# Batch 0's attention weights as zero-padded bands: 8 products over 128 keys for a unit instead of 24, and a new order

## The chip, the cores and the metric

The kernel runs on one core of one Trainium2 chip. The metric is the device time of one execution in microseconds (us). Three runs of the kernel before took 899.35, 900.56 and 900.95 us; the median is 900.56 us.

## The reference, cut to what matters

Attention over 8 batches, 8 heads, 576 positions, head size 64, with a causal window of 32 keys (heads 0 to 3) or 32 keys at a stride of 4 (heads 4 to 7), and then one expert of a mixture layer on the 4608 tokens: two fp32 products with a rational function between them.

```python
scores = scale * np.matmul(q, k.transpose(0, 1, 3, 2))
mask_plain = (rel >= 0) & (rel < window)                                # window = 32
mask_dil = (rel >= 0) & (rel < window * dilation) & (rel % dilation == 0)  # dilation = 4
attn = np.exp(scores - np.max(scores, axis=-1, keepdims=True))
attn = attn / (np.sum(attn, axis=-1, keepdims=True) + 1e-09)
attn_out = np.matmul(attn, v)
# x: (4608, 512), w_in: (512, 2048), w_out: (2048, 512)
h = x @ w_in
g = (a[0] + a[1] * h + a[2] * h * h + a[3] * h * h * h) / (1 + |b[0]| * |h| + |b[1]| * h * h + 1e-6)
out = g @ w_out
```

## The kernel before

**Attention.** The host reorders the positions of heads 4 to 7, so that both kinds of window become 32 neighbouring keys. A batch is 6 units; a unit is 4 heads (two pairs, named h and e below) by 192 queries. Its 192 queries are six blocks of 32, (r, i) with r in 0..1 and i in 0..2, and each block sees 64 keys, its own 32 and the 32 before. So all weights of a unit are 128 rows (4 heads by 32 queries) by 6 blocks of 64 keys, 384 columns. For a unit, `scores` makes 24 products of 64 by 32 by 64; `max`, `sub`, `exp`, `sum`, `recip` and `norm` are the softmax on DVE, ACT and POOL; `transposes` turns the 384 columns in three transposes on TensorE into one PSUM tile, `place` copies it to SBUF, and `av` multiplies with the values. In batch 0 `av` writes the result with the head's dimensions on the partitions, ready for the expert: one product of 64 keys, 64 dimensions and 32 queries for each block and head, 24 for a unit. The two r lie on the two halves of the partitions, so the values are stored for every block with its 64 keys, twice in all (`NV` = 768 columns).

**The expert.** Tokens are taken 512 at a time (9 groups, c = 0 to 8; the last is the 64 last positions of all batches), hidden features 128 at a time (16 slices), which makes 144 tiles. fp32 is split into a high and a low part, and each product is three (`mm` calls on xh, xl, wi; gh, gl, wo): `h` is 12 matmuls of 128x512, then a chain of some 12 operations on ACT, DVE and POOL gives g, and 4 `out` groups of 3 matmuls add to the results. The order of the runs is batch 0 with slices 0 to 7, batch 1 with all, batch 0 with 8 to 15, then batches 2 to 7 and the rest. Batch 0's six units must be done before the first tile; their q, k and values lie in the buffers of late weights (wi10 to wi15, wo10 to wo15). The weights come from HBM as 64-bit numbers and take five steps each on ACT, DVE and POOL.

**The order.** A planner (`Plan`) records every operation with the engines it may run on, and `ORDER`, a list of operation numbers, says in which order the first 1,700 or so are issued; behind the list a greedy rule with the ranks `LATE`, `DUE` and `SLACK` goes on. Each engine works its queue in that order. SP issues every DMA, in one queue. Where the planner thinks TensorE idle early on, `keep_busy` puts in matmuls that add nothing; `BUSY_FIRST` of them stand before the first scores.

**The last tiles.** After the last `h` come only `out` groups, and the results are copied and stored.

Of the kernel before, what the change touches and what calls it, by code (L numbers as in the profile page):

```python
# [9 lines left out]
F32 = mybir.dt.float32  # L10
# [10 lines left out]
P = 128  # L21
# [3 lines left out]
NU = 6  # L25
# [7 lines left out]
DUE = [(0.61, -8.7), (32, -0.49), (-84.45, -0.42), (274.73, 8.63), (68.21, 1.37), (195.45, 20.3), (123.08, 14.82), (125.28, 21.17)]  # L33

LATE = {"ab": -152.03, "ql": -170.47, "pl": 1.88, "qq": -9.41, "t1": 0.72, "t2": -587.38, "ln": -4.21, "ex": -485.44, "g0": -2.15, "g1": -1.06, "g2": -271.66, "gh": 7.36, "gl": 2.75, "out": 3.26}
SLACK = {"sc": 6.2, "qk0": -0.18, "v0": 4.16, "load": -25.39, "wi": 24.03, "wo": -4.42, "w": 3.79, "gl": -10.16, "out": 3.1}
# [3 lines left out]
BUSY_UNTIL, BUSY_LESS, BUSY_NS, BUSY_FIRST, KEEP = 150000.0, 250.0, 240.0, 14, 0  # L40
# [5 lines left out]
RQ, RKEY, NV, NMASK = 4 * 3 * 32, 4 * 128, 3 * 2 * 2 * 64, 6 * 32  # L46
# [23 lines left out]
0 2 3 6 1 18 32 7 20 8 9 10 21 102 11 34 22 35 12p 23 24 13 48 25 50 104p 36 14a 51 26p 37 38 96 39 97 103 15 64 16 114 27 52 53 17 28a 66 67 98p 54  # L70
40p 105 19 115 41 68 55 29 30 79 99 56p 81 69 42a 31 33 116a 57 58a 70p 43 5 4 82 83 138 140a 100d 288 84 117 44 71 290 106p 85 49 59 86 65 72a 291
299 139 46a 60 45 292 101p 141 293 87p 118a 294 295 73 126 88 74 80 62d 61 142p 289 301 310 302 296 127 89d 119p 75 297 77a 128p 298a 143d 303 304 129
305 306 90 174 312 318 76a 91 92 307 93d 107p 130p 319 150 313 151 94a 108 320 308 78 321 176p 326 300 131p 175 309a 322 1074 152p 109 120 110p 153
328 111 323 177 112d 1075 1076d 334 63 47 1077 324 178p 1079 335 122a 342 311 121 1078p 329 325a 162 336 1092 179p 344 1080 337 338 123 1081 1082 132
164p 339 1083 1084 1085 95 314 1093 163 351 113p 124a 340 1095 341a 359 144 1094p 352 1096d 134a 1099 133 353 1110 1097 1086p 165 1087p 330 327 1098
345 315 135 1100 145 354 1111 316 361 343 376 1112a 125p 1101 156 355 210 136p 1088 356 368 369 1102 1103 186 370 362 1089 317p 357 371 1090 1091 1113
358d 146a 1104a 372 373 1115 154p 166p 331 1114p 168 167d 1117 1105d 157 363 378 158a 374 360 375d 1116 1108 155p 147 159 1118 332 1119 170a 137p 395
198 1128 160a 385 1129 1130a 1120 161p 1121 379 386 1106 1109 1107 1132p 1131 364 1122a 1133 169 387 1135 1134 148a 1123p 1136 1146 171 1137 1138 1147
397 346 192 180 1139 1149 1125 1151 333p 188a 365 1124 1127 1148p 398 1150p 347 1140a 1164 377 1152 388 1126 1153 1141p 389 1154 181 149d 1142 182p
1165 1166a 399 1155 1167 366p 1156 380 396 1157 400 1168p 381 200a 1158a 1145 1144 1169 172p 1182 367 1170 1143 1159d 183 1163 1171 348 173p 1172 1173  # L80
390 187 184p 1183 1160 384 1184a 216 414 1174 1175 1185 401 1186p 1176a 1161 1187 1189 1188 1190 350 349p 189 1177d 382 1200 1201 193 1191 1192 1193
402p 1162 1202a 1203 383p 1204d 185p 194a 1179 1181 1180 1194a 1205 1206 403 1207 1208 1195d 195 1226 1178 1209 199 1227 1228a 201 1229 1230p 196a
1210 197p 211 1211 1212a 1231 1232 1233 1197 1234 1199 1198 1196 1213d 404 212p 1244 1215 1216 391 190a 1245 1246p 1248p 1247 1222a 1235 228 1236 1237
1238a 1217 1224a 1214 1249 405 1239p 1251 1220a 1250 1252 1218a 1262 213 1263 1243 1265 222 415 1253 204 191p 1223 1254 214a 202a 1255 1240 205 1267
1256a 1264p 1266p 1268 1257d 1241 392 1269 203p 234 1242 1270 1271 1280 1281 1282p 1272 223 1283 1221 1258 1260 393 1273 406 1285 217 224a 1286 1284p
1219 1274p 1287 1259 1261 235 1298 1288 1275d 1278 225 236p 1299 1300p 1289 407 1302p 1290 1276 246 1291 1301 1303 1304 1277 1279 408 206a 247 1225
1316 1292p 394 1293d 237 1297 1305 1306 270 1307 248a 207 1295 1296 1317 1318a 240 1294 1319 238a 1308 432 416 242p 1320p 1309 1310a 1321 226a 249 258
1323 1322 1324 230a 208p 422 1311p 259 1334 227p 1335 409 1337 1325 260a 1326 1327 1315 1328a 1336p 218a 1313 1338p 229 423 1339 1312 1340 1341 1342
1329d 261 1352 1330 219 1353 209p 1354a 1333 1314 1343 1344 1356p 1331 410 1332 1345 1355 282 262a 1370 1346a 1347p 1357 1358 239p 1359 252 424 1350
1360 1361 411 220a 1349 425 1362 1363 1371 1373 1372p 1374p 1351 1348 412 272a 1375 1376 231 1364a 1365d 1388 215p 1377 1378 1389 1391 254a 1368 1379  # L90
1390p 1380 241 1392p 426 1381 1382p 1393 1394 1367 427 1369 1366 1383d 253 243 250a 1395 433 1396 1397 428 221p 1406 1384 1398 1407 1399 244a 1408a
1385 1387 1409 1411 1412 1410p 1400a 1401p 1386 271 1424 273 1413 1414 1404 1403 251p 1415 413 264 232a 233p 1402 1405 1416 1417 265 1425 1427 1429
1426a 1428d 1442 1418a 276 1419p 1430 417 1423 1431 255 1432 1422 1420 1433 1434 263p 1421 245d 1443 434 1444a 1435 1446p 1445 1447 1448 266a 1436p
267 1437p 1449 1450 435 1460 256a 1438 1451 450 257d 1439 277 284a 1452 1453 278p 1461 1441 1463 274a 418 1454a 1465 440 1478 1466 469 1462p 441 429
1464p 1455p 279 1440 268p 1467 275p 1468 1469 1470 1471 1457 442 1479 1480a 1481 1472a 1456 443 1483 1484 1459 1458 1496 1482p 444 1485 280a 1473p
1486 269d 1476 1487 283 1477 1474 1497 281p 1488 1498p 1499 445 1475 1489 1490a 430 436 419 437 1500p 431 1501 1502 1491p 285 1503 1522 1504 1505 1523
1506 1493 1494 452 446 1525 1507 286a 1527 447 1528 1540 1508a 1524p 459 460 1526p 448 1495 1509p 1529 1530 287p 1531 1532 1541 420 1492 1542p 1533
1543 1544p 488 449 451 1534p 461 1545 421p 1546 1511 462 1535p 1510 1558 463 453 1513 507 1547 1548 1514a 1559 1516a 1549 1520a 464 1550 1515 1560p
# [1122 lines left out]
```

## Time and profile before

| | |
|---|---|
| median of three runs | 900.56 us |
| the profiled execution | 900.37 us |
| its span, first to last instruction | 898.3 us |
| TensorE (PE) busy | 882.3 us, 98%; 8172 matmuls |
| its weight loads (PEld) | 714.6 us, 80% |
| DVE, ACT, POOL busy | 716.1, 667.2, 502.5 us |
| share of the chain that ended last | PE 88%, DVE 4%, DMA 2%, ACT 2% |

TensorE is busy nearly all the time, so the span is the sum of what TensorE does and the few places where it stands still or runs at half its clock. "Busy" counts the matmuls of `keep_busy` too, and a matmul at half clock as twice the time; idle time of the other engines costs nothing by itself. A row of the timeline gives start, duration, engine, line, operation, output and input tile, count, and in brackets the idle time before it with what ended it; "issue" is a wait for nothing that the profile shows. An fp32 product of the attention is two MATMUL records, one of the expert is one, and each record has a LDWEIGHTS record of its own; the first tile's first matmul starts at 41.96 us, that of the ninth (batch 1's first) at 95.72 us.

### The profile page before, as it was taken

To read this page: it belongs to the slowest core of one execution; us is meant where nothing else is said; L and a number is where in the kernel's file an instruction comes from. 1 tells how busy PE (TensorE), PEld (TensorE's weight loads), DVE (VectorE), ACT (ScalarE), POOL (GpSimd) and SP (SyncE) were. 2 spreads that over 40 slices of the span, in tenths; PEclk is the share of its full clock that TensorE was granted. 3 is DMA by queue.
4 is the path that set the end of the run, shared out by engine and by line. 5 is a ranking of instruction groups with operands and counts; after the bars stand their busy time and mean duration, and the time that the engine had idled before them with its cause. 6 is when DMAs were issued, how large, how long until landed. Compare 5 with 4: busy or idle time off the path is not lost.

```text
span 898.3 us, 21077 instructions
## 1 busy us (share of the span) xinstructions
PE 882.3 (98%) x8172; PEld 714.6 (80%) x8172; DVE 716.1 (80%) x1272; ACT 667.2 (74%) x1111; POOL 502.5 (56%) x461
## 2 busy tenths in 40 slices
PE   7889999999999999999999999999999999999998
PEld 4767888887888788888888888888888888888886
DVE  4699999989889899999899778767766577667656
ACT  3699988875578777776776787777777688777765
POOL 3576767887665565554754564544554444444432
PEclk8799999999999999999999999999999999999999
DMA  9686553145765456555565114100100120001001
GB/s 354 245 292 213 181 203 103 50 122 175 228 193 151 142 188 196 170 170 168 157 204 179 46 36 129 30 0 1 48 19 1 44 71 0 1 1 48 1 0 48
DMA packets 85188, 103.45 MB, mean 115 GB/s; under 512 B 37216, under 2 KB 62560, under 8 KB 85088
## 3 DMA queue, kind: packets, MB, share of 16 engines
q1 hardware_dynamic: 85088, 102.11, 35.5%
q8 instruction: 64, 1.05, 0.5%
q14 instruction: 36, 0.29, 0.1%
HBM read 75.21 MB, written 26.87 MB: 114 GB/s over the span
## 4 chain that ended last, share of the span: by engine, by line
PE 88%; DVE 4%; DMA 2%; ACT 2%; issue 1%; SPq 1%; DVEq 0%; ACTq 0%
PE h L337 41%; PE out L337 41%; PE pair L337 5%; DMA left<-l 1%; DMA pT<-turned 1%; SPq L334 1%; DVE t L343 0%; DVE spare_h L346 0%; DVE a L346 0%; DVE t L346 0%; ACT p L340 0%; DVE h L346 0%; ACT t L340 0%; DVE wi L343 0%; ACT r L340 0%
## 5 line engine op out<-in xcount | busy, mean ns | idle before, releaser
L337 PE MATMUL h<-xh,wi 128*128 128x512 f32 x1136 | 375.9, 392 | 0.4 <-ACT pT L340 0.3
L337 PE MATMUL out<-gh,wo 128*128 128x512 f32 x1136 | 353.3, 392 | 0.7 <-ACT gh L340 0.7
L349 POOL TENSOR_TENSOR a<-r,a 128x512 f32<-128x512 f32 x137 | 178.0, 1299 | 226.5 <-ACT r L340 210.0
L337 PEld LDWEIGHTS h<-xh,wi 128*128 128x128 f32 x1136 | 213.2, 188 | 48.4 <-DVE a L346 1.3
L346 DVE SCALAR_TENSOR_TENSOR a<-a,h 128x512 f32<-128x512 f32 x280 | 191.7, 684 | 72.8 <-POOL gl L349 40.6
L337 PEld LDWEIGHTS out<-gh,wo 128*128 128x128 f32 x1136 | 211.3, 188 | 46.0 <-ACT gh L340 1.1
L337 PE MATMUL out<-gl,wo 128*128 128x512 f32 x568 | 221.3, 390 | 0.3 <-DVE gl L343 0.3
L337 PE MATMUL h<-xl,wi 128*128 128x512 f32 x568 | 221.5, 390 | 0.0
L349 POOL TENSOR_TENSOR gl<-a,gh 128x512 fp32r<-128x512 f32 x129 | 169.2, 1311 | 59.9 <-ACT gh L340 59.0
L340 ACT ACTIVATE a<-h 128x512 f32<-128x512 f32 x140 | 83.5, 596 | 102.4 <-PE h L337 101.9
L343 DVE TENSOR_TENSOR t<-t,h 128x512 f32<-128x512 f32 x142 | 96.6, 680 | 55.2 <-ACT t L340 54.9
L337 PEld LDWEIGHTS out<-gl,wo 128*128 128x128 f32 x568 | 106.6, 188 | 23.7 <-DVE gl L343 1.1
L337 PEld LDWEIGHTS h<-xl,wi 128*128 128x128 f32 x568 | 106.7, 188 | 21.4
L340 ACT ACTIVATE r<-a,ln_bias 128x512 f32<-128x512 f32 x141 | 100.8, 715 | 25.5 <-POOL a L349 24.9
L340 ACT ACTIVATE h<-r,exp_bias 128x512 f32<-128x512 f32 x142 | 98.1, 691 | 20.2 <-DVE t L346 16.2
L346 DVE SCALAR_TENSOR_TENSOR t<-t,na_t,h 128x512 f32<-128x512 f32 x142 | 105.9, 746 | 4.5
L340 ACT ACTIVATE t<-h,na_t 128x512 f32<-128x512 f32 x142 | 108.3, 763 | 1.5 <-PE h L337 1.5
L346 DVE SCALAR_TENSOR_TENSOR h<-t,na_t,h 128x512 f32<-128x512 f32 x142 | 105.9, 746 | 0.0
L340 ACT ACTIVATE r<-a,ab_t 128x512 f32<-128x512 f32 x121 | 98.8, 816 | 3.9
L340 ACT ACTIVATE gh<-a 128x512 fp32r<-128x512 f32 x129 | 80.9, 627 | 23.9 <-PE out L337 21.8
L349 POOL TENSOR_TENSOR p<-p,sm 128x384 f32<-128x384 f32 x42 | 35.8, 853 | 39.1 <-DVE sm L485 27.6
L349 POOL TENSOR_TENSOR xl<-z,xh 128x256 fp32r<-128x256 f32 (+5 forms) x55 | 40.4, 751 | 2.3 <-ACT xh L340 1.5
(124 smaller groups left out, 688.1 us busy)
## 6 DMA issues: line engine op xcount, KB each, us to landing
qk<-in_qk_dram SPq DMA_DIRECT2D x48, 448.0 KB, 5.3
v<-in_vp_dram SPq DMA_DIRECT2D x47, 384.0 KB, 3.9
out_dram<-os SPq DMA_DIRECT2D x36, 256.0 KB, 2.5
wi_raw<-in_w_in_dram SPq DMA_DIRECT2D x16, 512.0 KB, 7.9
wo_raw<-in_w_out_dram SPq DMA_DIRECT2D x16, 512.0 KB, 6.0
results<-y SPq DMA_DIRECT2D x42, 192.0 KB, 2.9
z<-results SPq DMA_DIRECT2D x168, 48.0 KB, 3.2
turned<-u SPq DMA_DIRECT2D x36, 192.0 KB, 2.1
```

Of the source, the lines that this page charges most:

```text
L334: pin(nc.sync.dma_start(dst, src))
L337: pin(nc.tensor.matmul(o, lhs, rhs, start=start, stop=stop, skip_group_check=free))
L340: pin(nc.scalar.activation(o, i, func, **kw))
L343: pin(nc.vector.tensor_tensor(o, x, y, op))
L346: pin(nc.vector.scalar_tensor_tensor(o, x, s, y, op0, op1))
L349: pin(nc.gpsimd.tensor_tensor(o, x, y, op))
```

## The change

A unit's normalised weights of batch 0 are now written into a buffer in which each block of 64 columns is followed by 96 zeros (`WAY` = 160). Read in steps of 128 columns, three blocks become three pieces of 128 keys by 32 queries in which the weights lie as a band among zeros, all against the same 128 keys. So `turn_band` makes two sets of three transposes (one for each r, each in a PSUM tile of its own), `place_band` two copies, and `av_band` 8 products: for each r, h and e one of 128 keys, 64 dimensions and 96 queries. The values are stored once for every 96 queries with 128 keys (`NBAND` = 512 columns, 1.33 times). The zeros and the turned weights lie in batch 1's still empty x tiles; a DVE memset of 1152 columns writes the zeros once, and batch 1's first copy into x waits for unit 5's products. `BUSY_FIRST` goes from 14 to 9, the matmuls that `transposes` put in front are gone, the planner's costs of an instruction fetch and of DMA are changed, and `ORDER`, `DUE`, `LATE` and `SLACK` hold new numbers.

```diff
-DUE = [(0.61, -8.7), (32, -0.49), (-84.45, -0.42), ...
+DUE = [(-79.11, 14.47), (58.02, -3.62), (48.26, 16.05), ...
-BUSY_UNTIL, BUSY_LESS, BUSY_NS, BUSY_FIRST, KEEP = 150000.0, 250.0, 240.0, 14, 0
+BUSY_UNTIL, BUSY_LESS, BUSY_NS, BUSY_FIRST, KEEP = 150000.0, 250.0, 240.0, 9, 0
+WAY, BANDS = 160, 2
 ORDER = """
-0 2 3 6 1 18 32 7 20 8 9 10 21 102 11 34 22 35 12p 23 24 13 48 25 50 104p 36 14a 51 26p 37 38 96 39 97 103 15 64 16 114 27 52 53 17 28a 66 67 98p 54
+1 3 0 4 21 7 37 23 8 9 10 11 109 2 24 39 12 25 55 26 6 13d 110 14 16 27 28 29p 40 41 57 15a 42 32 58 43 17a 115 116 117p 18 19 139 30 111p 44 73 112
...
-                self.v = pool.tile([P, NV], F32, tag=plan.at(tag), name=f"v{self.n}", bufs=1)
-                load(self.v, vp[self.n - 1])
+                self.v = pool.tile([P, NBAND if self.start else NV], F32, tag=plan.at(tag), name=f"v{self.n}", bufs=1)
+                load(self.v, vb[self.n - 1] if self.start else vp[self.n - NU])
...
         def new_p(self):
+            if self.start:
+                self.wide = bands["p"][:, plan.slot("pb")]
+                self.p = self.wide.rearrange("p (j m) -> p j m", m=WAY)[:, :, :64]
+                return
...
+        def turn_band(self, r):
+            t = psum.tile([P, 512], F32, tag=plan.at("h"), name=f"t{self.n}_{r}")
+            self.t[r] = t
+            for i in range(3):
+                first = 3 * WAY * r + P * i
+                pin(nc.tensor.transpose(t[:, P * i : P * i + P], self.wide[:, first : first + P], ident))
+
+        def place_band(self, eng, r):
+            self.pT[r] = bands["t"][:, plan.slot("pt")]
+            copy(eng, self.pT[r], self.t[r][:, :384])
+
+        def av_band(self):
+            v_t = self.v.rearrange("p (r h e d) -> p r h e d", r=2, h=2, e=2)
+            for r in range(2):
+                turned = self.pT[r].rearrange("p (i g q) -> p i g q", i=3, g=4)
+                for h in range(2):
+                    for e in range(2):
+                        mm(self.o_ps[64 * e : 64 * e + 64, r, 192 + 96 * h : 288 + 96 * h], v_t[:, r, h, e], turned[:, :, 2 * h + e], start=h == 0, free=True)
...
-                        if self.start:
-                            c0, c1 = 192 + 96 * h + 32 * i, P * i + 32 * g
-                            mm(self.o_ps[64 * e : 64 * e + 64, r, c0 : c0 + 32], v_t[half, i, h, e], self.pT[half, c1 : c1 + 32], start=i == h == 0, free=True)
...
+            if start:
+                self.t, self.pT, self.placed, turns = {}, {}, [], []
+                for r in range(2):
+                    tr = op({"PE": 480}, 0, lambda e, r=r: self.turn_band(r), no, identity, words=6, tail=-40)
+                    pl = op(BOTH, 0, lambda e, r=r: self.place_band(e, r), tr)
...
+                if b == 1:
+                    eh.follows.append(Unit.last_band)
...
+        pin(nc.vector.memset(bands["p"].rearrange("p b (j m) -> p (b j) m", m=WAY)[:, :, 64:], 0.0))
```

On TensorE, from the scores of unit 3 to the first transposes of unit 2. A name such as `qk3` is unit 3's q and k, `pT0` or `turned_bands` the turned weights, `t1` unit 1's transposes, and `x24` a row's count; before:

```order
L337 MATMUL pair_85<-qk3_242 32x64 x24
L337 MATMUL pair_B_99<-pT0_275,v0_112 64x32 x24
L500 MATMUL t1_322<-ident_90,p1_230 128x128 x3
L337 LDWEIGHTS ident_b_91
L337 MATMUL pair_A_98<-v0_112,ident_b_91 128x192
L337 LDWEIGHTS ident_b_91
L337 MATMUL pair_A_98<-v0_112,ident_b_91 128x192
L337 MATMUL pair_A_98<-qk4_315 32x64 x24
L500 MATMUL t2_370<-ident_90,p2_273 128x128 x3
```

and now:

```order
L341 MATMUL pair_85<-qk3_228 32x64 x24
L507 MATMUL t1_1_280<-ident_90,bands_112 128x128 x3
L341 MATMUL pair_B_99<-turned_bands_113,v0_115 64x96 x8
L507 MATMUL t1_0_307<-ident_90,bands_112 128x128 x3
L341 LDWEIGHTS ident_b_91
L341 MATMUL pair_A_98<-v0_115,ident_b_91 128x192
L341 LDWEIGHTS ident_b_91
L341 MATMUL pair_A_98<-v0_115,ident_b_91 128x192
L341 MATMUL pair_A_98<-qk4_314 32x64 x24
L507 MATMUL t2_0_351<-ident_90,bands_112 128x128 x3
```

Unit 1's second set of transposes is new, and unit 0's products are 8 of 96 queries where 24 of 32 stood.

A little further on TensorE, from unit 5's scores to unit 6's (batch 1's first); before:

```order
L337 MATMUL pair_85<-qk5_411 32x64 x24
L500 MATMUL t3_449<-ident_90,p3_326 128x128 x3
L337 MATMUL pair_B_99<-pT2_443,v2_446 64x32 x24
L500 MATMUL t4_498<-ident_90,p4_374 128x128 x3
L337 LDWEIGHTS ident_b_91
L337 MATMUL pair_85<-mask_t_89,ident_b_91 128x192
L337 LDWEIGHTS ident_b_91
L337 MATMUL pair_85<-mask_t_89,ident_b_91 128x192
L337 MATMUL pair_85<-qk6_492 32x64 x24
```

and now:

```order
L341 MATMUL pair_85<-qk5_374 32x64 x24
L507 MATMUL t3_1_418<-ident_90,bands_112 128x128 x3
L507 MATMUL t3_0_434<-ident_90,bands_112 128x128 x3
L341 MATMUL pair_B_99<-turned_bands_113,v2_376 64x96 x8
L341 MATMUL pair_A_98<-turned_bands_113,v3_422 64x96 x8
L507 MATMUL t4_1_483<-ident_90,bands_112 128x128 x3
L341 LDWEIGHTS ident_b_91
L341 MATMUL pair_85<-mask_t_89,ident_b_91 128x192
L341 LDWEIGHTS ident_b_91
L341 MATMUL pair_85<-mask_t_89,ident_b_91 128x192
L341 MATMUL pair_85<-qk6_443 32x64 x24
```

Unit 3's products have moved ahead of unit 6's scores, and unit 4's transposes come in two parts.

At the end of TensorE's queue, around the last tile's `h` (`h143`); before:

```order
L337 MATMUL out8_3_0_10235<-gh139_10638,wo11_2330 128x512 x2
L337 MATMUL out8_3_0_10235<-gl139_10642,wo11_2330 128x512
L337 MATMUL h143_10712<-xh8_9449,wi15_2553 128x512
L337 MATMUL h143_10712<-xl8_9450,wi15_2553 128x512
L337 MATMUL h143_10712<-xh8_9449,wi15_2553 128x512 x2
```

and now:

```order
L341 MATMUL out8_3_0_10180<-gh138_10540,wo10_2094 128x512 x2
L341 MATMUL out8_3_0_10180<-gl138_10544,wo10_2094 128x512
L341 MATMUL h143_10614<-xh8_9335,wi15_2216 128x512
L341 MATMUL h143_10614<-xl8_9336,wi15_2216 128x512
L341 MATMUL h143_10614<-xh8_9335,wi15_2216 128x512 x2
```

The last `h` has moved one `out` group forward: behind it stand the groups of tiles 139 to 143, where those of 140 to 143 stood.

## Rows read from the trace of the kernel before

**Rows 1.** Windows: stretch, then each engine's busy time with its count of instructions.

```profile
core 0: us, PE busy (x) PEld busy (x) DVE busy (x) ACT busy (x) POOL busy (x), PEclk, DMA share, GB/s
0.00:41.96 41.96, 33.88 (x847) 24.05 (x847) 21.62 (x59) 21.94 (x66) 18.65 (x33) 0.80 0.79 295
41.96:95.72 53.76, 51.06 (x679) 39.34 (x677) 51.11 (x91) 50.42 (x104) 37.32 (x38) 1.00 0.81 268
...
860.00:898.30 38.30, 33.62 (x145) 26.57 (x143) 22.66 (x33) 20.69 (x31) 11.64 (x9) 0.99 0.07 28
```

**Rows 2.** Windows from the start to 14.5, 21.2, 26 and 41.9 us.

```profile
0.00:14.50 14.50, 10.77 (x223) 5.62 (x224) 5.54 (x14) 3.71 (x6) 4.51 (x17) 0.97 0.87 327
0.00:21.20 21.20, 16.53 (x351) 9.76 (x351) 9.51 (x25) 7.96 (x22) 5.88 (x19) 0.84 0.92 350
0.00:26.00 26.00, 19.79 (x478) 12.37 (x479) 13.28 (x34) 12.12 (x34) 9.54 (x23) 0.87 0.94 360
0.00:41.90 41.90, 33.82 (x845) 23.99 (x846) 21.57 (x58) 21.88 (x66) 18.59 (x33) 0.80 0.79 294
```

**Rows 3.** Timeline of TensorE, 0 to 30 us.

```profile
1.46 5.76 PE L337 MATMUL pair_A<-ident_b 128*128 128x512 bf16 x14 [1.46 <-POOL ident_b masks.py:199]
...
7.31 0.72 PE L337 MATMUL pair_A<-qk 64*32 64x64 f32 x48
...
12.17 0.55 PE L500 MATMUL t<-ident,p 128*128 128x128 f32 x3 [1.63 <-POOL p L349]
...
13.46 0.40 PE L337 MATMUL pair_B<-pT,v 64*64 64x32 f32 x3
15.15 1.50 PE L337 MATMUL pair_B<-pT,v 64*64 64x32 f32 x45 [1.29 <-issue]
...
21.54 0.55 PE L337 MATMUL pair_B<-pT,v 64*64 64x32 f32 x23 [0.64 <-issue]
...
27.76 0.48 PE L337 MATMUL pair<-mask_t,ident_b 128*128 128x192 bf16 x2 [2.96 <-POOL p L349]
```

**Rows 4.** Windows, TensorE alone: stretch, length, busy, granted clock, DMA share, GB/s.

```profile
14.00:20.00 6.00, 4.85 (x103) 0.50 1.03 403
...
28.00:37.00 9.00, 9.00 (x209) 0.50 0.31 121
```

**Rows 5.** Timeline of TensorE, 23 to 42 us, at the full clock.

```profile
23.42 0.90 PE L337 MATMUL pair_B<-pT,v 64*64 64x32 f32 x48
...
38.65 0.73 PE L337 MATMUL pair<-v,pT 64*32 64x64 f32 x48
39.31 0.34 PE L337 MATMUL pair<-mask_t,ident_b 128*128 128x192 bf16 x2
...
40.24 0.61 PE L337 MATMUL pair_A<-xh,minus 128*128 128x64 f32 x3
40.96 0.92 PE L337 MATMUL pair<-mx,ident 128*128 128x192 f32 x4
41.72 0.49 PE L500 MATMUL t<-ident,p 128*128 128x128 f32 x3
41.96 0.48 PE L337 MATMUL h<-xh,wi 128*128 128x512 f32 x1
```

**Rows 6.** DMA issues: tiles, count, KB each, us to landing.

```profile
v<-in_head_dram SPq DMA_DIRECT2D x1, 483.0 KB, 3.9
```

**Rows 7.** Groups by line and form: weight loads (PEld) of the transposes; busy us, mean ns.

```profile
L500 PEld LDWEIGHTS t<-ident,p 128*128 128x128 f32 x36 | 4.7, 164 | 4.4 <-POOL p L349 1.8 <-ACT wo L340 1.2 <-issue 0.4
```

**Rows 8.** Timeline of ACT: unit 0's turned weights copied to SBUF.

```profile
12.75 0.49 ACT L340 ACTIVATE pT<-t 128x384 f32<-128x384 f32 x1 [0.64 <-PE t L500]
```

**Rows 9.** Timeline of SP's queue, 22 to 37 us.

```profile
22.88 0.33 SPq L334 DMA_DIRECT2D wo_raw<-in_w_out_dram  x1
36.63 0.39 SPq L334 DMA_DIRECT2D left<-l  x1
```

**Rows 10.** Timeline of TensorE, the last tile's out groups.

```profile
891.22 0.73 PE L337 MATMUL out<-gh,wo 128*128 128x512 f32 x2 [0.69 <-ACT gh L340]
```

More of the change, by code (lines that the diff above doesn't have):

```diff
@@ L74 @@
[L74 to L77, printed above, removed]
@@ L160, in at, with slot @@
         return tag if len(self.tags[tag]) == 1 else f"{tag}_{self.now[tag]}"
+    def slot(self, tag):
+        return self.now[tag]
     def held(self, o, eng):
@@ L433, in p_blocks @@
         def p_blocks(self):
-            order = "p (i r) k -> p r i k" if self.by_pe else "p (r i) k -> p r i k"
+            order = "p (i r) k -> p r i k" if self.by_pe and not self.start else "p (r i) k -> p r i k"
             return self.p.rearrange(order, r=2)
@@ L506, in new_pT @@
         def new_pT(self):
-            if self.start:
-                self.pT = work.tile([P, 512], F32, tag=plan.at("a"), name=f"pT{self.n}", bufs=1)[:, :384]
-            elif self.n % 2:
+            if self.n % 2:
                 self.pT = att.tile([P, 6, 64], F32, tag=plan.at("p"), name=f"pT{self.n}").rearrange("p j k -> p (j k)")
@@ L653, in plan @@
             lq = op({"SP": 430}, 0, lambda e: self.load_qk(qp, qt), dma=(RQ + RKEY) * 512)
-            self.lv = lv = op({"SP": 430}, 0, lambda e: self.load_v(vpool, self.vt), dma=NV * 512)
+            self.lv = lv = op({"SP": 430}, 0, lambda e: self.load_v(vpool, self.vt), dma=(NBAND if start else NV) * 512)
             prev, clear = None, []
@@ L714, in plan @@
                 early.extend((lq, lv))
-            for o in (sc, ma, mx, su, ex, sm, rc, no, tr, *self.placed, *([sb] if kind == 2 else [])):
+            for o in (sc, ma, mx, su, ex, sm, rc, no, *(turns if start else [tr]), *self.placed, *([sb] if kind == 2 else [])):
                 o.slack = 0.0
@@ L721, in plan @@
             plan.takes(sc, self.s_tag, 1, [su, *clear])
-            plan.takes(su, "p", PS, [tr])
+            if start:
+                su.deps.append(zeroed)
+                plan.takes(su, "pb", BANDS, turns)
+            else:
+                plan.takes(su, "p", PS, [tr])
             plan.takes(mx, "mx", 2, [sb if kind == 2 else su])
@@ L773, in finish @@
             if start:
-                plan.takes(self.placed[0], "a", A, [av])
+                Unit.last_band = av
+                for pl in self.placed:
+                    plan.takes(pl, "pt", 2 * BANDS, [av])
                 plan.takes(av, self.o_tag, 1, [x for x in (el, kl) if x])
@@ L1070, in memsets, with zero_bands @@
         pin(nc.gpsimd.memset(exp_bias, -LOG_SHIFT * 0.6931471805599453))
+    bands = {}
+    def zero_bands():
+        bands["p"] = xpool.tile([P, BANDS, 6 * WAY], F32, tag="xh" + x_slot(1), name="bands")
+        bands["t"] = xpool.tile([P, 2 * BANDS, 384], F32, tag="xl" + x_slot(1), name="turned_bands")
+        pin(nc.vector.memset(bands["p"].rearrange("p b (j m) -> p (b j) m", m=WAY)[:, :, 64:], 0.0))
+    zeroed = op({"DVE": 1300}, -88, lambda e: zero_bands())
     identity = op({"POOL": 1300}, -89, lambda e: make_idents())
@@ L1187 @@
     vw = vw.reshape(B, 2, 2, 2, 3, 2, 3, 2, 32, D)
-    vs = vw[:BY_PE].transpose(0, 1, 4, 5, 7, 8, 6, 2, 3, 9).reshape(BY_PE * NU, P, NV)
+    vk = np.stack([vpad[0, :, :, :, 96 * n : 96 * n + 128] for n in range(6)], axis=3).reshape(2, 2, 2, 3, 2, P, D)
+    vk = vk.transpose(0, 3, 5, 4, 1, 2, 6).reshape(NU, P, NBAND)
+    vs = vw[1:BY_PE].transpose(0, 1, 4, 5, 7, 8, 6, 2, 3, 9).reshape((BY_PE - 1) * NU, P, NV)
     vr = vw[BY_PE:].transpose(0, 1, 4, 5, 8, 7, 6, 2, 3, 9).reshape((B - BY_PE) * NU, P, NV)
```

119 lines of the change are left out of this document (61 added, 58 removed).

## The prediction

> **What bounds the kernel now.** I read the windows first. From the first tile's h (41.96 us) to batch 1's first (95.72 us) TensorE is idle for 53.76 - 51.06 = 2.70 us, and in the last 38.30 us for 4.68 [rows 1]; between them the table's 98% leaves next to nothing. Behind the first h the change adds no work to TensorE and takes none away; the same nine scores, seven products and eight units' transposes stand ahead of it in both orders. So the time changes by three terms: the start of the first h, the idle time up to 95.72, and the end.
>
> The next view is TensorE's timeline of the start. In 41.96 us it is busy for 33.88 at a mean clock of 0.80 [rows 1]. The reader is to see three holes: after the first three of unit 0's products it stands still until 15.15 (1.29 us of "issue"), again 0.64 us before 21.54, and 2.96 us before 27.76 [rows 3]. The page gives the last to a POOL result, but the record counts say otherwise: the holes come after 447, 702 and 957 LDWEIGHTS and MATMUL records, exactly 255 apart [rows 2]. I read them as waits for the instructions themselves: TensorE runs out of code. 1691 records stand ahead of the first h.
>
> The third view is the granted clock: 0.50 from 14 to 20 us and from 28 to 37 [rows 4], so 1.2 instead of 2.4 GHz, each time after a hole with TensorE standing, and back to full after a stretch of unbroken work.
>
> **The change part by part.** The profiled execution took 900.37 us, 0.19 less than the median of 900.56; the sum is made against it, and 2.07 of it lie outside the span of 898.3.
>
> The start. Five of the 14 first dummies go, at 5.76 / 14 = 0.41 us each, 2.1 us [rows 3]. The first scores would start at 5.2; their data, landing 3.9 us after the issue [rows 6] near 5.1 us, allows that, so 5.5 instead of 7.31. The softmax behind it moves with it, and unit 0's transposes start near 10.4 instead of 12.17 [rows 3]. The next limit is the first hole, which by the order falls again inside unit 0's products. If fetching moves with the program it ends at 13.4, if by the wall clock at 15.15 as now [rows 3]. The DMA engines are saturated then (share 1.03 [rows 4]) and no copy of code comes earlier for a shorter program, so I take 14.6, nearer the wall clock: -0.55.
>
> From the end of that hole to the first h, before: 41.96 - 15.15 = 26.8 us. At the full clock the work would take: six units' products at 0.90 [rows 5], 5.4; seven units' transposes at 0.4 (0.49 by the row's duration, 0.24 from its start to the h behind it [rows 5]), 2.8; five masks with scores, 40.24 - 39.31 = 0.93 each [rows 5], 4.65; three subtractions on TensorE at 41.72 - 40.96 = 0.76 [rows 5], 2.3; unit 6's products 0.66 (38.65 to 39.31); less twice, 1.1; two dummies 0.8. That is 17.7. The holes add 3.6. The rest, 5.5, is the half clock: some 16.5 us at 1.2 GHz, 0.33 us for each.
>
> After, the same pieces with two changes. Unit 0 to 5's products become 8 fp32 products over 96 queries. No row shows this form. A record of 192 columns takes 0.76 / 4 = 0.19 us [rows 5], so one of 96 at least 0.095, and 16 records 1.5 us one after the other. Bounds: the two e use different columns of the array; if they run together, 0.76. If each weight load, half of the 164 ns of 128 columns [rows 7], stands ahead of its product uncovered, 16 x (0.095 + 0.082) = 2.8. I take 1.3, near the subtraction's rows: 7.8 for six against 5.4, a loss of 2.4. And eleven sets of three transposes stand behind the hole instead of seven: 4.4 against 2.8. Without the two dummies the sum at the full clock is 7.8 + 4.4 + 4.65 + 2.3 + 0.66 + 1.1 = 20.9. By work alone the change loses 3.2 us.
>
> What it gives back are records: 1691 less 384 (six units, 96 to 32 each), less 14 (seven dummies), plus 36 (six more sets of transposes) is 1329. The holes would fall where 702, 957 and 1213 records have passed: in the scores of units 5, 7 and 8. A product that takes 81 ns a record (1.3 / 16) where 0.90 / 96 = 9 ns stood [rows 5] runs through code nine times slower; in 0.9 us of such products 96 records passed, now 11. So the next block has time to arrive, and I take the later holes as gone: -3.6. The half clock after 28 us followed the hole of 2.96 us; without it I leave only the first stretch, 3.0 instead of 5.5: -2.5.
>
> New waits. Each unit's turned weights are two copies of 0.49 us [rows 8] on ACT or DVE, and its products wait for both. Other units' scores and transposes lie between, so I take 0.5 us in all, between 0 and 2. The zeros (a DVE memset of 1152 columns, the engine's first work) lie beside the first dummies and cost nothing; if they ran late, the first unit's subtraction would wait for them. Batch 1's copy into x waits for unit 5's products, which in the order are past before the first h.
>
> So the first h starts at 14.6 + 20.9 + 3.0 + 0.5 = 39.0: 41.96 - 39.0 = -3.0 us.
>
> From the first h to batch 1's. SP works in order: it stood idle between wo0's transfer at 22.88 and a `left` store at 36.63 [rows 9], which waits for unit 4's result and holds up the weights behind it. In the new order the store of unit 3 is at that place (both the 25th transfer), so weights come earlier; six units' values are 256 instead of 384 KB, 0.79 MB or about 2 us at 403 GB/s [rows 4]. Against that the stretch is nearly full: DVE 51.11 us with 91 instructions, 0.56 each, and ACT 50.42 of 53.76 [rows 1]. I take -0.5 (from -2.7, all idle time gone, to +2).
>
> The end. The last h has one more tile's out groups behind it: 12 matmuls of 33.62 / 145 = 0.23 us each [rows 1], 2.7 us more cover for the last chain. The wait of 0.69 us before the last outs [rows 10] and a shorter one ahead of it, 0.25, go: -0.9 (0 if the copies behind come late).
>
> Sum: -3.0 - 0.5 - 0.9 = -4.4: the profiled time becomes 896.0, and by the median 896.2. Own range 893 to 899.8: the products between 0.76 and 2.8 would move the sum by -3.2 and +9, of which I keep +2 in it, and the first hole by 1.2.
>
> **Rivals.**
>
> The holes stay as they are, since they may not come from the record count. For it: the page names POOL for the longest one. Against: three gaps all 255 records apart. Then 2.4 + 1.6 us of work come on top, less 0.8 for dummies and 0.9 at the end and some of the start: about 900. Chance 0.08. The Trainium skill's "Runtime: NRT & Kernel Launch", section "Instruction fetch mechanics", has code arriving in blocks of 256 instructions and calls crossing into the next mostly hidden. The trace agrees on the block and not on the hiding: 1.29 + 0.64 + 2.96 = 4.9 us in three crossings [rows 3]. By the page fewer records would give nothing.
>
> The half clock holds. If TensorE runs the whole stretch at 1.2 GHz, since the new products come one at a time with gaps for copies, 14.6 + 21.4 become 14.6 + 33.4, with 0.36 us more for each at half clock: the first h at 48.0, +6.0, and with the end +5: 905. It decides from about 20 us at half clock on. For it: 15 of 28 us between 14 and 42 are at 0.50 today [rows 4]. Against: both stretches follow a hole. Slower; chance 0.10.
>
> The weight loads stay uncovered: 2.8 instead of 1.3 us for a unit, 9 us more, about 905. For it: the old products used two halves of 64 rows in turn, the new ones all 128. Against: in the last 38.30 us, PE is busy for 33.62 and the loads for 26.57 [rows 1], all of 128 rows, so these do overlap. Slower; chance 0.08. The Trainium skill's "TensorE: Matmul & The Clock Gate", section "The mechanism" under Part 3, says that a weight load runs beside matmuls in flight only where the row groups differ, which speaks for this rival; the rows of the end disagree.
>
> The gain is given back before batch 1. By 95.72 the order has seven more instructions on DVE, 7 x 0.56 = 3.9 us [rows 1], on an engine that is busy for 95% of the stretch. If batch 1's tiles wait for it, 899.5. Chance 0.10.
>
> It goes better: 0.76 us for a unit's products, no half clock after 20 us and no idle time behind the first h: about 892. Chance 0.10.
>
> **How the numbers follow.** The forecast has 0.54, the rivals 0.46. A measurement of this kernel can tell about 0.2% from no change, so "same" is 898.8 to 902.4. Faster: 0.48 of the forecast's 0.54, the better case, and 0.06 of the holes and the given-back gain: 0.64. Same: 0.06 of the forecast and 0.10 of those two: 0.16. Slower: clock and weight loads, and 0.02 of the given-back gain: 0.20. The range takes the better case nearly whole and half of the slower ones: 891.5 to 903.
>
> **What would show it.** Right: first scores near 5.5 us, the first h near 39, unit 0's products ending about 1.3 us (or 81 ns a record) from their start, no "issue" hole at 702, 957 or 1213 records, a granted clock near 1.00 from 22 us on, under 2.5 us of idle time between the first h and batch 1's, no wait before the last outs. Wrong: a clock of 0.50 from 14 us to the first h, products at 170 ns a record, holes after the same counts, or batch 1's first h more than 54 us behind the first.

## The result, and the profile after

The changed kernel takes 891.59 us, the median of four runs (891.10 to 892.78), against 900.34 us for the kernel before beside it: a ratio of 0.9906, with a 95% interval of 0.9889 to 0.9923. In a second comparison it was 893.07 against 901.19 us, 0.9913 (0.9899 to 0.9927). So 8.1 to 8.8 us went, where 4.4 had been forecast. The profiled execution took 891.10 us, its span 889.1; the span of before was 898.3, 9.2 us longer.

The windows of the changed kernel, with the same columns as [rows 1], cut at its own first h, at batch 1's first and at the end:

```profile
0.00:35.16 35.16, 28.50 (x666) 20.01 (x666) 27.47 (x67) 23.34 (x69) 15.79 (x30) 1.00 0.97 363
35.16:85.48 50.32, 48.34 (x670) 37.81 (x668) 48.54 (x89) 46.89 (x101) 35.58 (x38) 1.00 0.72 235
850.00:889.10 39.10, 35.03 (x154) 28.35 (x152) 21.95 (x32) 20.65 (x32) 12.92 (x10) 1.00 0.07 27
```

The first h starts at 35.16 us instead of 41.96. This is 6.80 of the 9.2 us. The stretch from there to batch 1's first h is 50.32 us long instead of 53.76, mostly because three `out` groups, 9 matmuls, now come later; its idle time on TensorE is 50.32 - 48.34 = 1.98 us (2.70 before), with DVE and ACT as full as they were. Most of the rest is at the end. TensorE's timeline there, the 24 empty products that fill the wait for the last chain and the last of all:

```profile
876.98 5.60 PE L341 MATMUL out<-spare_l,wo 128*128 128x512 f32 x24
...
884.91 0.39 PE L341 MATMUL out<-gl,wo 128*128 128x512 f32 x1
```

From the first of the 24 to the last matmul it is 7.93 us; before it was 9.19 (884.93 to 894.12), for the same matmuls. The wait of [rows 10] is gone, and with it 1.26 us.

TensorE's timeline of the start, to be held against [rows 3] and [rows 5]:

```profile
5.79 0.72 PE L341 MATMUL pair_A<-qk 64*32 64x64 f32 x48
...
10.71 0.85 PE L507 MATMUL t<-ident,bands 128*128 128x128 f32 x6 [1.18 <-DVE bands L347]
...
13.82 0.88 PE L341 MATMUL pair_B<-turned_bands,v 128*64 128x96 f32 x15 [0.42 <-issue]
...
17.13 0.88 PE L341 MATMUL pair_B<-turned_bands,v 128*64 128x96 f32 x16 [0.65 <-issue]
...
20.07 0.34 PE L341 MATMUL pair<-qk 64*32 64x64 f32 x13 [0.92 <-issue]
...
21.15 0.88 PE L341 MATMUL pair_B<-turned_bands,v 128*64 128x96 f32 x16
21.88 0.88 PE L341 MATMUL pair_A<-turned_bands,v 128*64 128x96 f32 x16
23.34 0.52 PE L507 MATMUL t<-ident,bands 128*128 128x128 f32 x3 [0.58 <-DVE bands L347]
...
35.16 0.48 PE L341 MATMUL h<-xh,wi 128*128 128x512 f32 x1
```

The reader is to see three things. A unit's 8 products take 21.88 - 21.15 = 0.73 us from start to start. Two waits for code are left, 0.42 us and, in the middle of unit 5's scores, 0.92, where 1.29, 0.64 and 2.96 stood. And there are new waits ahead of a unit's work, as 0.58 us before unit 4's transposes and 0.65 before unit 1's products; what ended the latter the profile does not name. The counts up to the two waits for code, against [rows 2]:

```profile
0.00:13.80 13.80, 10.12 (x222) 5.53 (x223) 7.25 (x17) 4.55 (x9) 3.76 (x16) 1.00 0.86 317
0.00:20.05 20.05, 14.80 (x349) 9.22 (x350) 13.14 (x31) 9.06 (x20) 7.75 (x20) 1.00 0.91 343
```

222 + 223 and 349 + 350 records have passed, where 447 and 702 had in [rows 2]. The windows leave out the semaphore instructions of TensorE's own queue, 4 and 6 of them here, 2 and 3 in the kernel before; with these the waits lie behind 449 and 705 records in both kernels. Behind 961, where the kernel before stood for 2.96 us, the changed one does not stand at all. The counts 449, 705, 961, 1217 and 1729, here and below, have the semaphore instructions in them.

That these are waits for code, the profile shows by itself: a DMA queue of the kind `instruction`, q8, moves packets of 16 KB, 62 of them in the changed kernel (15982 LDWEIGHTS and MATMUL records) and 64 in the kernel before (16344), so one for some 256 records. Its row between 12.6 and 13.8 us of the kernel before, and between 11.3 and 12.5 us of the changed one (packets, MB, share of 16 engines):

```profile
q8 instruction: 1, 0.02, 5.4%
...
q8 instruction: 1, 0.02, 5.3%
```

In the kernel before, such packets end at 13.70, 20.08 and 26.18 us, each 1.5 to 1.6 us ahead of the end of a wait (15.15, 21.54, 27.76); in the changed one they end at 12.40 and 18.81 us, 1.4 and 1.3 us ahead of 13.82 and 20.07. Its third packet ends at 25.08, and TensorE comes to the record behind 961 only at 27.21, so it does not wait there.

The granted clock, against [rows 4], over the same stretches:

```profile
14.00:20.00 6.00, 4.50 (x127) 1.00 1.04 400
28.00:37.00 9.00, 8.31 (x157) 1.00 1.04 385
```

No stretch of the start is at half clock. SP's queue, as [rows 9]:

```profile
21.32 0.33 SPq L338 DMA_DIRECT2D wi_raw<-in_w_in_dram  x1
26.98 0.39 SPq L338 DMA_DIRECT2D left<-l  x1
```

It is blocked for 5.7 us, not 13.7, behind an earlier `left` store.

### The profile page after: what moved, and what is told of

It reads as the page before. It is cut to its first block, busy times and chain, and to the rows that moved or that the text cites. A ratio compares the mean times of both kernels' runs of the same rounds, so it can differ in the third digit from the quotient of the medians.

```text
span 889.1 us, 20736 instructions
## 1 busy us (share of the span) xinstructions
PE 875.1 (98%) x7991; PEld 710.0 (80%) x7991; DVE 722.9 (81%) x1285; ACT 661.4 (74%) x1104; POOL 499.7 (56%) x462
## 4 chain that ended last, share of the span: by engine, by line
PE 84%; DVE 7%; ACT 4%; DMA 2%; issue 1%; POOL 1%; SPq 0%; DVEq 0%; ACTq 0%; POOLq 0%
PE out L341 40%; PE h L341 39%; PE pair L341 5%; DVE a L350 1%; ACT r L344 1%; DVE h L350 1%; ACT p L344 1%; PE pair_A L341 1%; DMA pT<-turned 1%; DVE xl L347 1%; ACT xh L344 1%; DVE t L347 0%; DMA results<-y 0%; DVE sm L489 0%; DVE wo_f L350 0%
## 5 line engine op out<-in xcount | busy, mean ns | idle before, releaser
L353 POOL TENSOR_TENSOR a<-r,a 128x512 f32<-128x512 f32 x133 | 172.6, 1298 | 253.3 <-ACT r L344 230.1
L353 POOL TENSOR_TENSOR gl<-a,gh 128x512 fp32r<-128x512 f32 x134 | 177.3, 1323 | 41.9 <-ACT gh L344 40.0
L344 ACT ACTIVATE h<-r,exp_bias 128x512 f32<-128x512 f32 x142 | 98.2, 691 | 21.2 <-DVE t L350 15.0
L353 POOL TENSOR_TENSOR xl<-z,xh 128x256 fp32r<-128x256 f32 (+5 forms) x58 | 42.5, 748 | 9.9 <-ACT xh L344 8.5
L353 POOL TENSOR_TENSOR p<-p,sm 128x384 f32<-128x384 f32 x36 | 31.0, 861 | 12.1 <-DVE sm L493 9.1
```

Of the source, the lines that this page charges most:

```text
L344: pin(nc.scalar.activation(o, i, func, **kw))
L353: pin(nc.gpsimd.tensor_tensor(o, x, y, op))
```

## The experiments

"First h" is where the first tile's h starts in the profiled execution of each. The ratio is to runs of the kernel before on the same chip.

| kernel | median us | ratio, 95% interval | first h, us |
|---|---|---|---|
| before, again | 900.94 | 0.9998 (0.9984 to 1.0012) | 40.71 |
| before, 9 empty matmuls first | 901.49 | 1.0005 (0.9995 to 1.0015) | 40.56 |
| before, wait ahead of unit 0 filled | 901.86 | 1.0007 (0.9998 to 1.0016) | 42.93 |
| before, long hole filled | 902.98 | 1.0018 (1.0005 to 1.0031) | 44.41 |
| changed, again | 893.07 | 0.9913 (0.9899 to 0.9927) | 35.74 |
| changed, 24 products | 902.31 | 1.0006 (0.9990 to 1.0021) | 42.48 |
| changed, loops exchanged | 893.61 | 0.9916 (0.9888 to 0.9943) | 36.38 |
| changed, halves apart | 893.44 (one run) | | 35.57 |
| changed, 128 rows | 894.59 (one run) | | 38.17 |
| changed, 14 first | 894.53 | 0.9914 (0.9890 to 0.9937) | 35.60 |
| changed, 2 first | 894.30 | 0.9910 (0.9894 to 0.9927) | 35.80 |
| changed, values of 384 KB | 894.87 | 0.9913 (0.9892 to 0.9934) | 35.65 |

**24 products over the bands.** Each product of 96 queries becomes three of 32; order, copies and values stay as changed.

```diff
-                    for e in range(2):
-                        mm(o_ps[.., 192 + 96 * h : 288 + 96 * h], v_t[:, r, h, e], turned[:, :, 2 * h + e], ...)
+                    for i in range(3):
+                        for e in range(2):
+                            mm(o_ps[.., c0 : c0 + 32], v_t[:, r, h, e], turned[:, i, 2 * h + e], ...)
```

> The changed kernel, with each product of 96 queries cut into three of 32: 24 products over 128 keys for a unit, 48 records instead of 16, the same bands, copies, values and order. Theory: the waits for code come from records passed too quickly; with 192 more records ahead of the first h a unit's products again run through the code in 0.8 to 1 us, the waits after 447, 702 and 957 records grow to 3.5 to 5 us in all, the clock falls to 0.50 behind one of them, and the first h starts at 38.5 to 42 us: 895 to 899 us. Rival: the gain comes from the new order and the earlier start, not from the number of products: first h within 1 us of 35.2, 891 to 892.5 us.

The first h starts at 42.48 us and the time is that of the kernel before. Its windows up to three of the waits and to just before the first h, then TensorE's timeline and clock behind the wait at 25.71:

```profile
0.00:19.50 19.50, 14.35 (x349) 9.23 (x350) 11.33 (x27) 7.77 (x15) 6.33 (x18) 1.00 0.91 339
0.00:25.70 25.70, 18.75 (x476) 13.10 (x477) 17.09 (x40) 12.03 (x32) 10.57 (x24) 1.00 0.94 355
0.00:42.40 42.40, 33.82 (x856) 26.22 (x857) 29.07 (x70) 25.40 (x72) 17.58 (x32) 0.96 0.83 304
```

```profile
25.71 0.31 PE L341 MATMUL pair_B<-turned_bands,v 128*64 128x32 f32 x4 [1.78 <-issue]
25.84 2.49 PE L341 MATMUL pair_A<-turned_bands,v 128*64 128x32 f32 x48
...
42.45 0.27 PE L527 MATMUL t<-ident,p 128*128 128x128 f32 x1 [1.43 <-ACT wi_f L853]
```

```profile
26.00:29.40 3.40, 3.40 (x54) 0.53 0.86 334
```

A third wait for code, 1.78 us, stands where 476 + 477 records have passed, 961 with the semaphore instructions, and the clock behind it is 0.53: the 48 records of unit 3 take 2.4 us there, and 1.52 at the full clock (33.28 to 34.80). The 1.43 us before the first h lie behind 1729 records by the start times, five times 256 more than 449; the name in the brackets is not what ended them. So all of the gain at the start hangs on the products' form. New order, earlier start and smaller values together, without it, give nothing that can be measured. But this run alone does not part the number of records from the products' own time: six units at 1.52 instead of 0.73 us are 4.7 of the 7.3 us by which the first h comes later, without any wait.

**What sets 0.73 us.** First the loops over h and e were exchanged.

```diff
-                for h in range(2):
-                    for e in range(2):
+                for e in range(2):
+                    for h in range(2):
```

> The changed kernel, with the two loops of a unit's 8 products exchanged: the four products of one r come as two on the first 64 columns of TensorE's array and then two on the other 64, not in turn. Same records, same order of everything else. Theory: products take 0.73 us a unit (start to start) because two neighbours on different columns run at the same time; exchanged, three quarters of the pairs that overlap now no longer do, a unit's products take 1.1 to 1.5 us, six units cost 2 to 4.5 us, the first h starts at 37 to 39.5 us instead of 35.2, and the whole takes 893 to 896 us. Rival: a record of 96 columns takes 0.046 us by itself, whichever columns it is on: 0.73 us a unit, 891.6 us as before the exchange.

A unit took 0.80 us (22.69 to 23.49), not 1.1 or more: by this run alone the theory of overlapping halves would fall. Its first h is 0.6 to 1.2 us later, but a late load of q and k (1.27 us before unit 4's scores) and a spell of half clock behind it account for that. The exchange proved too mild: most records still start in pairs. So all four products of one half were put ahead of the other four.

```diff
+            for e in range(2):
+                for r in range(2):
+                    for h in range(2):
```

> The changed kernel, with all four products of a unit that write the first 64 rows ahead of all four that write the other 64, so that only one pair of neighbours in eight has different columns of the array. Theory A (two products on different columns run at the same time): 16 records of 0.08 us with little overlap, 1.15 to 1.3 us a unit. Theory B (the two records of one product run at the same time, whichever columns; the next product follows 0.08 us later): 0.73 to 0.8 us a unit.

The products' groups by line and form, first of the changed kernel, then with the halves apart (busy us, mean ns of one):

```profile
L341 PE MATMUL pair_B<-turned_bands,v 128*64 128x96 f32 x64 | 3.8, 252 | 1.1 <-issue 1.1
...
L341 PE MATMUL pair_A<-turned_bands,v 128*64 128x96 f32 x32 | 1.8, 252 | 0.0
```

```profile
L341 PE MATMUL pair_B<-turned_bands,v 128*64 128x96 f32 x64 | 5.2, 252 | 1.5 <-issue 1.5
...
L341 PE MATMUL pair_A<-turned_bands,v 128*64 128x96 f32 x32 | 2.5, 252 | 0.2 <-ACT turned_bands L344 0.2
```

96 records are busy for 7.7 us instead of 5.6. A unit's record starts show why: four follow one another at 82 to 83 ns, eight come in pairs with 82 ns for each two, and four are alone again; in the changed kernel all sixteen come in pairs, in four of the six units 6 to 7 ns apart, and 82 ns from pair to pair. So one record of 96 queries is 82 ns, and two products run at the same time when they use different 64 columns of the array. The sum is about 1.1 us a unit: theory A, a little under the 1.15 to 1.3 that it gave, since eight records still found a partner. Which two records make a pair, the profile does not say.

**128 rows.** The same 8 products with the values of two heads as weights.

```diff
-                        mm(self.o_ps[64 * e : 64 * e + 64, r, ...], v_t[:, r, h, e], ...)
+                        mm(self.o_ps[:, r, ...], v_t[:, r, h].rearrange("p e d -> p (e d)"), ...)
```

> The changed kernel, with each of a unit's 8 products made with the values of both heads of a pair as 128 weight columns, so that it writes 128 rows where 64 are wanted; the other 64 are overwritten with what the reference does not ask for, so this kernel leaves out the right result of half the heads in batch 0. Theory B: with 128 columns of weights the two records of a product have no columns left to share and follow one another as in the subtraction's rows: 16 x 0.08 = 1.3 us a unit, the figure that the forecast took, and the first h 2 to 4 us later than with 64 rows (37.5 to 40 us). Theory A: two products in turn can no longer overlap either, 1.3 us; if the time is set by the number of records alone, 0.73 to 0.85 us a unit.

```profile
L341 PE MATMUL pair_B<-turned_bands,v 128*128 128x96 f32 x64 | 8.0, 276 | 1.6 <-issue 1.6
...
L341 PE MATMUL pair_A<-turned_bands,v 128*128 128x96 f32 x32 | 3.9, 274 | 0.0
```

11.9 us of busy time for 96 records, one after the other at 111 to 112 ns: 1.8 us a unit, more than the 1.3 that I had expected, and the first h at 38.17. Nothing is left to run beside, and each record shows some 30 ns beyond the 82.

**The clock and the holes.** In the kernel before, 6 matmuls that add nothing fill the 1.63 us in front of unit 0's transposes.

```diff
-                keep_busy(KEEP, self.t)
+                keep_busy(6 if self.n == 0 else 0, self.t)
```

> The kernel before, with 6 matmuls of 128x512 that add nothing put in front of unit 0's transposes, where TensorE stands still for 1.63 us. Theory A: the clock falls near 14 us because of this standing; filled, the granted clock stays 1.00 until about 21 us, which gives back about 6 us x 0.33 = 2 us: 898 to 899 us. Theory B: the clock falls because of the first hole (1.29 us without code) and those behind it: the clock still falls to 0.50 near 14 to 15 us, 12 more records move the holes a little, 900 to 901 us.

```profile
14.39 0.30 PE L337 MATMUL pair<-qk 64*32 64x64 f32 x3 [1.54 <-issue]
...
20.51 0.66 PE L337 MATMUL pair_B<-pT,v 64*64 64x32 f32 x29 [0.89 <-issue]
...
26.74 0.42 PE L337 MATMUL pair_B<-pT,v 64*64 64x32 f32 x3 [3.35 <-issue]
```

```profile
15.00:20.00 5.00, 4.62 (x114) 0.66 1.03 401
27.00:39.00 12.00, 12.00 (x245) 0.50 0.36 119
```

Theory B: filling the wait did not keep the clock up (0.66 from 15 to 20 us). It falls behind the hole that ends at 14.39 and again behind the 3.35 us before 26.74. Then 18 such matmuls were put in front of unit 3's transposes, ahead of the long hole.

```diff
-                keep_busy(KEEP, self.t)
+                keep_busy(18 if self.n == 3 else 0, self.t)
```

> The kernel before, with 18 matmuls of 128x512 that add nothing (4.1 us at the full clock) in front of unit 3's transposes, so that TensorE works where it stood still for 2.96 us. It has more to do, and 36 more records. Theory: the half clock from 28 to 37 us follows that standing; filled, the clock is 1.00 from 22 us on, which gives back about 9 x 0.36 = 3.2 us while the filling costs about 1.2 us more than the hole: first h at 39 to 40.5 us, 899 to 900.5 us where the kernel before takes 901. Rival: the half clock comes from the kind of work there (many small products) and not from the standing: first h at 42.5 us or later, 902 us or more.

TensorE's timeline, the clock of two stretches, and the count up to the wait before 32.88:

```profile
21.91 4.06 PE L337 MATMUL t<-ident_b 128*128 128x512 bf16 x18
...
32.88 1.30 PE L337 MATMUL pair_B<-pT,v 64*64 64x32 f32 x41 [2.17 <-issue]
...
43.90 0.43 PE L337 MATMUL pair<-mx,ident 128*128 128x192 f32 x1 [0.89 <-issue]
...
44.41 0.48 PE L337 MATMUL h<-xh,wi 128*128 128x512 f32 x1
```

```profile
21.00:30.00 9.00, 8.75 (x226) 1.00 1.03 406
32.90:39.50 6.60, 6.60 (x131) 0.50 0.16 19
```

```profile
0.00:32.80 32.80, 25.91 (x605) 16.46 (x606) 16.68 (x47) 14.57 (x40) 12.96 (x26) 0.90 0.89 343
```

The time of this kernel I had wrong: it is 0.18% slower, since two new holes (2.17 and 0.89 us) came, behind 1217 and 1729 records. But the place was right: the clock is 1.00 from 21 to 30 us, where it was 0.50 behind the old hole, and falls to 0.50 right behind the new one. From 26 us on the first stretch holds the units' own small products, as the second does, so the kind of work is not the cause; what differs is the standing. In both of these runs, filling a hole with empty work only moved it.

**The start.** The kernel before with 9 empty matmuls first, the planner's numbers unchanged.

```diff
-            return keep_busy(BUSY_FIRST if since == Plan.PE_START else ...
+            if since == Plan.PE_START:
+                keep_busy(9, o.spare)
+                return BUSY_FIRST
+            return keep_busy(...
```

> The kernel before, with 9 instead of 14 matmuls that add nothing ahead of the first scores, and its own order. Theory: code arrives a fixed time (about 6.2 us) after TensorE has passed record 150, so the first hole moves forward with the program: first scores at 5.8 instead of 7.3, the hole ends at 13.8 instead of 15.15, the first h starts 1 to 2 us earlier, 898.5 to 899.5 us. Rival: the hole ends by the wall clock near 15.15 whatever stands ahead, and the five matmuls only lengthen it: 900.3 us. A third: fewer matmuls ahead let the clock fall earlier: 901 us or more.

```profile
13.09 0.78 PE L340 MATMUL pair_B<-pT,v 64*64 64x32 f32 x40 [1.09 <-issue]
...
19.33 0.84 PE L340 MATMUL pair_B<-pT,v 64*64 64x32 f32 x18 [2.36 <-issue]
...
25.55 0.94 PE L340 MATMUL pair<-qk 64*32 64x64 f32 x45 [0.27 <-issue]
...
31.74 0.75 PE L340 MATMUL pair_B<-pT,v 64*64 64x32 f32 x18 [1.23 <-issue]
...
40.56 0.48 PE L340 MATMUL h<-xh,wi 128*128 128x512 f32 x1
```

```profile
13.00:19.00 6.00, 3.70 (x128) 0.97 1.03 403
19.30:25.00 5.70, 5.67 (x127) 0.50 1.03 401
```

The first hole ends at 13.09 instead of 15.15, so it moves with the program, as theorised; but the next is 2.36 instead of 0.64 us, and the clock falls behind it. The time is unchanged. The first h at 40.56 says nothing by itself, since the unchanged kernel's lies at 40.71 in another execution:

> The kernel before, unchanged, profiled beside the next three. Expected: holes after 447, 702 and 957 records, clock 0.50 behind them, first h near 42 us (41 to 43), 900 to 901.5 us. If its first h lies elsewhere, the profiles of other variants are to be compared with this one, not with the first.

```profile
27.48 0.48 PE L337 MATMUL pair<-mask_t,ident_b 128*128 128x192 bf16 x2 [2.96 <-POOL p L349]
...
40.71 0.48 PE L337 MATMUL h<-xh,wi 128*128 128x512 f32 x1
```

There the first h is 1.25 us earlier: 0.28 of it stands already at the end of the long hole, and behind that the clock came back sooner (0.93 from 33 us to the first h); 1.1 us of waiting for `pT` between 200 and 300 us, where [rows 1]'s execution had 0.5, took part of it back. One profile is good to about a microsecond at the first h. With 14 and with 2 empty matmuls first, by the same edit, the changed kernel shows the same from the other side:

> The changed kernel, with 14 instead of 9 matmuls that add nothing ahead of the first scores. Theory: what stands ahead of the first scores moves everything behind it, the holes too, since code comes a fixed time after a record: the first h starts 1.2 to 1.6 us later (36.4 to 36.8), 892.8 to 893.3 us. Rival: the start is paced by the loads (qk1 and qk4 come late), which do not move: the first h moves by less than 0.5 us, 891.6 to 892 us.

> The changed kernel, with 2 instead of 9 matmuls that add nothing ahead of the first scores, so TensorE stands still from about 2.3 us to the landing of unit 0's data near 5 us. Theory: the first scores start at 5.0 to 5.4 us in any case (they wait for data), 14 fewer records push the holes back a little, and if standing still lets the clock fall, a stretch from 5 us on shows 0.50 and the first h starts 0.5 to 2 us later: 892 to 893.6 us. Rival: the clock stays at 1.00, first h within 0.4 us of 35.2, 891.3 to 891.9 us.

First h at 35.60 and 35.80, ratios of 0.9914 and 0.9910: no difference that can be told. With 14 the first scores start 0.66 us later (6.45), with 2 unit 0's data are waited for until 5.07; the wait behind 705 records ends at 20.57 and at 20.72. What is saved ahead of a hole is lost in it. Both also pay for standing: with 14, a stand of 1.70 us before the first transposes is followed by a clock of 0.60 from 11 to 15 us; with 2, the first two units' scores behind a stand of 2.57 us take 0.97 us each, not 0.72, though the granted clock of these rows reads 1.00.

**The values' size.** Units 1 to 5 with 256 unused columns more.

```diff
-                self.v = pool.tile([P, NBAND if self.start else NV], ...)
+                self.v = pool.tile([P, NV], ...)
...
+                self.v = self.v[:, :NBAND] if self.start else self.v
```

> The changed kernel, with the values of units 1 to 5 padded with 256 unused columns, so each is transferred as 384 KB, as before the change, instead of 256: 0.66 MB more, 1.6 us at 400 GB/s. Theory A: the DMA engines are full until the first h and q and k of units 4 to 8 lie behind these values in the queue, so their scores wait: first h 1 to 2 us later, 892.5 to 893.6 us. Theory B: the waits that end last in this stretch are those for code and for the copies; the loads have slack: first h within 0.4 us, 891.4 to 892 us.

```profile
14.33 0.88 PE L341 MATMUL pair_B<-turned_bands,v 128*64 128x96 f32 x15 [1.08 <-issue]
...
20.56 0.34 PE L341 MATMUL pair<-qk 64*32 64x64 f32 x13 [1.46 <-issue]
...
35.65 0.48 PE L341 MATMUL h<-xh,wi 128*128 128x512 f32 x1
```

Theory B for the loads: behind 8 us no unit's scores wait for their q and k. Both waits for code end 0.5 us later than in the first profile, and the first h too; the unchanged kernel's second profile has 35.74, so this is within its scatter.

**The changed kernel again.**

> The changed kernel, unchanged, once more, to see what of its time belongs to one execution. Expected: waits for code at records 449 and 705, ending near 13.8 and 20.1 to 20.7 us, granted clock 1.00, first h at 35 to 35.8 us, 891.5 to 894 us, ratio 0.990 to 0.992. If the 2.4 us that the first profile gains behind the first h belong to the change, the stretch from the first h to the last out group takes 849 to 850 us again; if they are scatter of the waits for the round trip through HBM between 200 and 330 us, it takes 850.5 to 853 us, as in the variants.

From the first h to the start of the last matmul it takes 851.3 us here and 849.8 in the first profile, which by what was expected speaks for scatter; but the kernel before took 852.2 and 853.6, and so scatters as much, 1.5 us. All 14 profiles together say more: the changed kernel and its variants take 849.8 to 852.8 us, 851.1 in the mean, the kernel before and its variants 852.2 to 853.6, 853.1 in the mean. So about 2 us behind the first h belong to the change, 1.26 of them at the end. By the second profiles the first h gained 40.71 - 35.74 = 4.97 us, not 6.80. No run pointed to a version better than the changed kernel.

## Why the prediction was right or wrong

Direction, place and mechanism were right: three terms, the start by far the largest, the code waited for at every 256 records, and fewer records as the cure. The range from 891.5 held the time, only just. The size was half of what came: -4.4 against -8.75, and nearly all of the error is in one term, the first h, forecast at 39.0 and found at 35.16 (35.74 in the second profile). What came is nearly the case that I had called "it goes better", 892 us, with a chance of 0.10: its products and its clock came, the idle time behind the first h stayed at 1.98 us.

- **A unit's products: the step that failed.** "I take 1.3, near the subtraction's rows." It is 0.73, under the lower bound of 0.76, and that bound's reason, the two e on different columns run together, is the true one (halves apart: 1.1 us; 128 rows: 1.8). The subtraction has 128 weight columns, so no two of its records can share the array, and its row was the wrong neighbour. The nearer one stood in [rows 5]: the old products, 48 records in 0.90 us, which no serial reading allows. Six times 0.57 is 3.4 us of the error.
- **The half clock.** "I leave only the first stretch, 3.0 instead of 5.5." Nothing was left. The first hole is 0.42 instead of 1.29 us, and the clock stayed at 1.00. Here the spell of half clock went with the hole, and I had taken only one of the two spells away: 3.0 us, the second step that failed.
- **The end of the first hole.** "I take 14.6, nearer the wall clock." It was 13.82; the hole moves with the program (13.09 in the kernel before with 9), and the packet of code came earlier too, at 11.38 instead of 12.65 us. 0.8 us. But the runs with 2, 9 and 14 empty matmuls show that this term alone gives nothing.
- **The later holes.** "I take the later holes as gone." The one behind 961 records is; the one behind 705 is 0.92 us. The "nine times slower" that I gave for it set unlike counts side by side: 1.3 us over 16 are MATMULs alone, 0.90 over 96 are both kinds of record. Like for like my 1.3 us gave 41 ns against 9, and the 0.73 us measured give 23. The wait left over and the waits ahead of a unit's work (0.65, 0.58 and 0.44 us where I took 0.5 in all) went against the forecast, by 2.1 us, and hid part of the other errors. The rest, 1.3 us, also against it, lies in the other pieces of the sum, and which ones stays open.
- **Loads and SP.** I had put -0.5 on SP being freed and on smaller values. Idle time went by 0.7 us up to batch 1's first h; the size of the values showed no effect, and what SP's shorter wait did no run tests.
- **The end.** -0.9 forecast, -1.26 found, for the reason given.

Of the rivals, the kept holes fell (their places are counted in records in every kernel here, the packets of code end just ahead of them, and 24 products bring them back), the uncovered weight loads fell (with 128 columns a record takes 30 ns more; whether that is its weight load no run shows), and the half clock did decide, on the other side: it left.

## What to carry to other kernels

Price a new form of product by a row that uses the same part of the array: here two products of 64 columns, on different halves, ran side by side, and one of 128 columns had nobody beside it. Where small instructions go by faster than code arrives (here 256 records in some 6.2 us), count records, not busy time: fewer and larger ones paid twice here, by the wait and by the half clock that followed it. A saving ahead of such a wait is worth nothing until the wait itself shrinks.

## What the runs showed of the hardware that I had not expected

- The waits for code lie behind 449, 705, 961, 1217 and 1729 records of TensorE, to the record, in every kernel that reaches them too early, 256 or a multiple of it apart. In the start, where one wait follows another at the next 256 records, it ends 6.1 to 6.5 us after the one ahead of it: 15.15, 21.54 and 27.76 us in the kernel before, 13.82 and 20.07 in the changed one, 13.09, 19.33, 25.55 and 31.74 with 9 empty matmuls first; once it was 5.6 (24 products, 13.95 to 19.53).
- The 14 empty matmuls of the start took 5.76 us in one execution of the kernel before and 5.11 in a variant (wait ahead of unit 0 filled), although nothing ahead of them differs; the first start 0.43 us apart and the later ones 0.22, and the turn came behind 12 of them in the one and behind 9 in the other. The granted clock in the rows is 1.00 all along.
- Standing still for 1.46 us (values of 384 KB, before 20.56) was not followed by a half clock; 1.29 us in [rows 3] and 0.92 us in the kernel before with the long hole filled (0.61 from 14.4 to 20.5 us), both with 1.63 us of standing shortly ahead, were. What the clock goes by between these, the runs don't settle.
